# A half row of w2 in eight transfers instead of four, and small work moved off VectorE, in a fused decode step (attention cache and MLP) on one Trainium2 core

## The chip, the cores and the metric

The kernel runs on one core of a Trainium2 chip. The core has TensorE (PE, with its weight loads shown apart as PEld), VectorE (DVE), ScalarE (ACT), GpSimd (POOL) and SyncE (SP), and 16 DMA engines that move data between HBM and the on-chip SBUF. The metric is the device time of one launch in microseconds (us), the median of several runs. The profile is of one execution; its span runs from the first to the last instruction.

## The reference

One decode step for a batch of 2 with one query token each: attention over a cache of 4096 positions, and a GELU MLP, mixed by a gate. Everything is float32.

```python
B, Sq, D = 2, 1, 576
H, Sk, Dh = 32, 4096, 128        # k_cache, v_cache: [B, H, Sk, Dh], 134 MB each
F = 4608                         # w1: [D, F], w2: [F, D], wq: [D, H*Dh], wo: [H*Dh, D]

def _A_ref(x, k_cache, v_cache, wq, wo):
    q = (x @ wq).reshape(B, Sq, H, Dh).transpose(0, 2, 1, 3)
    scores = jnp.einsum("bhqd,bhkd->bhqk", q, k_cache) * (Dh ** -0.5)
    p = _softmax(scores, axis=-1)
    o = jnp.einsum("bhqk,bhkd->bhqd", p, v_cache)
    return o.transpose(0, 2, 1, 3).reshape(B, Sq, H * Dh) @ wo

def _B_ref(x, w1, b1, w2, b2):
    h = _gelu(jnp.einsum("bsd,df->bsf", x, w1) + b1)
    return jnp.einsum("bsf,fd->bsd", h, w2) + b2

g = _sigmoid((x * gate_w).sum(-1, keepdims=True))
return g * _A_ref(...) + (1 - g) * _B_ref(...)
```

## The kernel before

All weights and the whole cache go once through one SBUF tile, `ring`, of three slots of 64 KB a partition. `seq` lists the loads in their order: wq in two pieces and w1 in three, then for each of N = 16 units (one batch entry, four heads) a K block and a V block of 8.39 MB, and last w2 and wo in three groups (`LAST`). `load()` issues the next one on SP's queue. A slot is filled again when the instructions that read it are done. The order of instructions on each engine is that of the code (`manual_schedule`); the framework adds the semaphore waits.

For each unit i, DVE multiplies the K block by the query (`mul`, L510), POOL and DVE reduce it to scores (`red`, L514 to L516), PE and DVE find the maximum (`max_p`, `max_t` with the scaled identity `idsc`, `max_n`), ACT takes the exponentials into the tile `p` and their sums into `rs` (`softmax`, L535), and PE multiplies them with the V block (`av`, L546). That runs one unit behind the products. The front part computes the gate (L270 to L285), the query (L303 with `qps`), and the MLP's hidden layer (L303 with `hps`, L390 to L405), which leaves `hg`, [128 partitions, 36 rows, 2]. The hidden unit that belongs to partition p and row r is 36 p + r, and w2 is read in the same way: row r of w2's tile holds in partition p the weights of unit 36 p + r.

At the end `LAST` brings w2 and wo:

```python
LAST = (
    (("w2", 0, 14), ("w2", 14, 28)),
    (("w2", 28, 36), ("wx", 0, 1), ("wo", 0, 8), ("wo", 8, 16)),
    (("wo", 16, 23), ("wo", 23, 27), ("wo", 27, 30), ("wo", 30, 31), ("wo", 31, 32)),
)
```

Each entry is a transfer of 128 partitions, except that wo's last row comes in four column pieces, and `wx`: this is the second half (288 of 576 columns) of w2's row 35. It is laid out on 16 partitions with XS = 8 weight rows each instead of 128 with one. It is loaded by XC = 4 transfers (L155), each to 4 of the 16 partitions. To multiply it, the 128 x 2 values of `hg`'s row 35 have to be regrouped into `hx`, [16 partitions, 8, 2]: `hx[q, s] = hg[8 q + s, 35]`. Before, DVE does this with two reductions of the identity (`mod`, a mask of p mod 8, and `div`, a mask of p div 8) and a product, PE with one matmul, and DVE copies the result (L407 to L418). `mlp_x` (L421) then multiplies `hx` with `wx` on PE after the other rows of w2, and before wo (`wo_out`, `last_out`).

What sets when a transfer may be issued, beside its slot: the program has eight semaphores for the completion of transfers (named DMAHW0 to DMAHW7 in the rows below), and the transfers of SP's and ACT's queues take them in turn, in the order of the code. A transfer that takes a semaphore again waits until the transfer that had it eight places earlier has landed. SP issues its transfers one after the other, so what stands behind a waiting one waits too.

Of the kernel before, what the change touches and what calls it, by code (L numbers as in the profile page):

```python
# [8 lines left out]
F32 = mybir.dt.float32  # L9
AF = mybir.ActivationFunctionType  # L10
ALU = mybir.AluOpType
AX = mybir.AxisListType
P = 128
# [6 lines left out]
def kernel(  # L20
# [14 lines left out]
    nc = tc.nc  # L35
    B, H, SK, DH = k_cache.shape
# [21 lines left out]
    NF = F // P  # L58
# [4 lines left out]
    SCALE = float(DH) ** -0.5  # L63
# [26 lines left out]
    ps_sm = ctx.enter_context(tc.tile_pool(name="ps_sm", bufs=3, space=bass.MemoryType.PSUM))  # L90
# [18 lines left out]
    def load_w(w, rows, c):  # L109
        if c < len(rows):  # L110
            n = rows[c] * w.shape[1]
            lo = sum(rows[:c]) * P
            src = w[lo:lo + rows[c] * P].rearrange("(p r) n -> p (r n)", r=rows[c])
        else:
            n = w.shape[1] // 2
            src = w[NX * P:].rearrange("q (e n) -> (q e) n", e=2)
        t = ring[:, used["w"]:used["w"] + n]
        used["w"] += n
        nc.sync.dma_start(t, src)
        return t  # L120

    def slot(n):
        k = len(held) % SLOTS
        return ring[:, k * SLOT:k * SLOT + n]

    def load_heads(src, i):

        t = slot(SLOT)
        h = i // B * E
        nc.sync.dma_start(t, src[i % B, h:h + E].rearrange("h (p r) d -> (h p) (r d)", p=PE_))  # L130
        return t.rearrange("p (r d) -> p r d", d=DH)
# [3 lines left out]
    XE, XC = 4, 4  # L135
    XP = XE * XC
    XS = P // XP
    srcx2 = w2.rearrange("(e c s r) n -> c r e s n", e=XE, c=XC, s=XS)[:, NF - 1, :, :, DS:]

    def length(w, a, z):  # L140
        return XS * DS if w == "wx" else (z - a) * D - (DS if (w, z) == ("w2", NF) else 0)

    def load_last(m):
        n = sum(length(*q) for q in LAST[m])

        used["e"], used["z"] = len(held) % SLOTS * SLOT + n, (len(held) % SLOTS + 1) * SLOT
        t = slot(n)
        o = 0
        for w, a, z in LAST[m]:
            if w == "wx":  # L150
                xt = t[:XP, o:o + XS * DS]
                rows[w] = xt.rearrange("p (s n) -> p s n", s=XS)
                o += XS * DS
                for c in range(XC):
                    nc.sync.dma_start(xt[c::XC].rearrange("e (s n) -> e s n", s=XS), srcx2[c])  # L155
                continue
            if (w, z) == ("w2", NF):
                nc.sync.dma_start(t[:, o:o + length(w, a, z)], srcs[w][:, a * D:z * D - DS])
                for r in range(a, z):
                    rows[w, r] = t[:, o + (r - a) * D:o + min((r - a + 1) * D, length(w, a, z))]  # L160
                o += length(w, a, z)
                continue

            ends = (a * D, a * D + DS, a * D + DS + DO, z * D) if (w, z) == ("wo", 32) else (a * D, z * D)
            for u, v in zip(ends, ends[1:]):
                nc.sync.dma_start(t[:, o:o + v - u], srcs[w][:, u:v])
                o += v - u
            for r in range(a, z):
                rows[w, r] = t[:, o - (z - r) * D:o - (z - r - 1) * D]

    def temp(n, parts=P):
        t = ring[:parts, used["t"]:used["t"] + n]
        used["t"] += n
        assert used["t"] <= SLOTS * SLOT
        return t
# [7 lines left out]
    def load():  # L183
        if not seq:
            return
        kind, i = seq.pop()
        if kind == "wq":
            wqt[i] = load_w(wq, ROWS[kind], i)
        elif kind == "w1":
            w1t[i] = load_w(w1, ROWS[kind], i)  # L190
        elif kind == "k":
            kt[i] = load_heads(k_cache, i)
        elif kind == "v":
            vt[i] = load_heads(v_cache, i)
        else:
            load_last(i)
        if kind in ("k", "v", "last"):
            held.append((kind, i))
# [28 lines left out]
    ident = cp.tile([P, P], F32, name="ident")  # L227
    make_identity(nc, ident)
    ones = cp.tile([P, 1], F32, name="ones")
    nc.vector.memset(ones, 1.0)  # L230
    idsc = cp.tile([P, P], F32, name="idsc")
    nc.vector.tensor_scalar_mul(idsc, ident, SCALE)


    NPB = 1
# [3 lines left out]
    pt = []  # L239
    for j in range(NPB):  # L240
        t = cp.tile([P, NT * EB + 32 - EB], F32, name=f"p{j}")
        nc.vector.memset(t, 0.0)
        pt.append(t)
    rs = cp.tile([P, NO], F32, name="rs")
    nc.vector.memset(rs, 0.0)


    sel = ident.rearrange("p (j c) -> p j c", j=4)[:, :, :EB].rearrange("p j (e r) -> p j e r", e=E)
# [70 lines left out]
    to = temp(HG * NO).rearrange("p (f o) -> p f o", f=HG)  # L319
# [69 lines left out]
    for m, ps in enumerate(hps):  # L389
# [7 lines left out]
    hg = cp.tile([P, NF, B], F32, name="hg")  # L397
    t = temp(NF * B).rearrange("p (r b) -> p r b", b=B)
# [5 lines left out]
    nc.vector.tensor_mul(t, t, hb)  # L404
    nc.vector.tensor_mul(hg, t, g1.unsqueeze(1).to_broadcast([P, NF, B]))  # L405

    mod = temp(XS)  # L407
    nc.vector.tensor_reduce(mod, ident.rearrange("p (q s) -> p s q", s=XS), AX.X, ALU.add)
    div = temp(XP)
    nc.vector.tensor_reduce(div, ident.rearrange("p (q s) -> p q s", s=XS), AX.X, ALU.add)  # L410
    hm = temp(XS * B).rearrange("p (s b) -> p s b", b=B)
    nc.vector.tensor_mul(
        hm, hg[:, NF - 1:].to_broadcast([P, XS, B]), mod.unsqueeze(2).to_broadcast([P, XS, B])
    )
    hxps = ps_sm.tile([XP, XS * B], F32, tag="sm", name="hxps")
    nc.tensor.matmul(hxps, div, hm.rearrange("p s b -> p (s b)"), start=True, stop=True)
    hx = cp.tile([XP, XS, B], F32, name="hx")
    nc.vector.tensor_copy(hx.rearrange("p s b -> p (s b)"), hxps)  # L418
    load()

    def mlp_x():  # L421
        for s in range(XS):
# [232 lines left out]
```

## Time and profile before

| | before |
|---|---|
| median of 3 runs | 722.17 us (722.10 to 722.34) |
| profiled execution, its own time | 722.19 us |
| its span | 720.0 us |
| mean granted TensorE clock | 0.663 |
| moved by DMA | 308.84 MB, 429 GB/s over the span |
| busy: DVE, PE, POOL, PEld, ACT | 72%, 33%, 20%, 10%, 5% |

The profile's page shows the busy share of each engine in 40 equal slices, in tenths, and with it the share of the 16 DMA engines. Its DMA queues are q1 (SP's), q10 (ACT's) and two for instructions; packets counts every contiguous piece moved and every write to a completion semaphore. The chain of work that ended last is followed back from the last instruction. The timeline lists instructions by start and duration in us; SPq is SP's queue, and a DMA row there is the issue of a transfer, not its data. A row of windows gives for a stretch of time the busy time of PE, PEld, DVE, ACT and POOL with the number of instructions, then the granted clock, the DMA share and GB/s. A packet is counted in the window in which it starts, so that a share may be over 1.

### The profile page before, as it was taken

The page shows a single profiled execution, that of the slowest core. Times are in us where ns is not written, and L with a number is a line of the kernel's source. Part 1 is how long each engine was busy: PE and PEld are TensorE (multiplying, and loading weights), DVE is VectorE, ACT ScalarE, POOL GpSimd, SP SyncE. Part 2 cuts the span into 40 slices and gives each one's busy share as a digit, 9 for nine tenths or more (in the row PEclk, how much of TensorE's full clock was granted, in tenths as well). Part 3 has the DMA queues.
Part 4 walks back from the last instruction along what each step waited for, and adds up shares of the span by engine and source line. Part 5 has one row for each costly group of instructions (what it writes and reads, how often), then busy time and mean ns, then how long its engine had stood idle before and what let it go on. Part 6 is the DMA issues. An engine that isn't in the chain of part 4 may idle for free.

```text
span 720.0 us, 3946 instructions
## 1 busy us (share of the span) xinstructions
PE 235.7 (33%) x1681; PEld 72.8 (10%) x1681; DVE 518.3 (72%) x154; ACT 37.8 (5%) x141; POOL 143.2 (20%) x28
## 2 busy tenths in 40 slices
PE   0646013140516060604143140506070503223188
PEld 0322000010101010101010010101010101000023
DVE  0003969879696969696969879696969596978900
ACT  0010010100001010101010100101010101010000
POOL 1000040404050403022140404040503113040400
PEclk9967557575757575566657575757575665757599
DMA  9999999999999999999999999999999999999997
GB/s 409 412 443 434 433 437 419 451 420 448 426 448 420 437 437 419 442 430 441 434 433 441 430 431 433 437 430 431 441 430 444 427 444 426 433 430 438 415 426 303
DMA packets 7245, 308.84 MB, mean 429 GB/s; under 512 B 814, under 2 KB 1326, under 8 KB 1596
## 3 DMA queue, kind: packets, MB, share of 16 engines
q1 hardware_dynamic: 7204, 308.55, 99.2%
q8 instruction: 13, 0.21, 0.1%
q10 hardware_dynamic: 24, 0.05, 0.0%
q14 instruction: 4, 0.03, 0.0%
HBM read 308.59 MB, written 0.00 MB: 429 GB/s over the span
## 4 chain that ended last, share of the span: by engine, by line
DMA 45%; DVE 35%; PE 17%; ACT 1%; issue 1%; POOL 0%; ACTq 0%; DVEq 0%; SPq 0%; POOLq 0%
DMA ring<-in_A_k_cache_dram 34%; DVE ring L510 19%; DVE s L515 10%; PE av L546 10%; DMA ring<-in_B_w_dram 5%; DVE s L516 5%; DMA ring<-in_gate_w_dram 3%; DMA ring<-in_A_wo_dram 3%; PE hps L303 2%; PE qps L303 1%; ACT p L535 1%; PE oall L564 1%; DMA ring<-in_B_b_dram 1%; PE mt L525 1%; PE acc L367 1%
## 5 line engine op out<-in xcount | busy, mean ns | idle before, releaser
L510 DVE TENSOR_TENSOR ring<-ring,q 128x16384 f32<-128x16384 f32 x16 | 275.6, 17224 | 100.2 <-DMA ring<-in_A_k_cache_dram 100.2
L514 POOL TENSOR_TENSOR ring<-ring 128x3968 f32<-128x3968 f32 x16 | 137.0, 8564 | 486.9 <-DVE ring L510 419.1
L515 DVE TENSOR_REDUCE s<-ring 128x66 f32<-128x8448 f32 x16 | 143.2, 8953 | 1.3
L546 PE MATMUL av<-ring,p 128*32 128x512 f32 x1024 | 132.6, 676 | 11.4 <-ACT p L535 6.1
L525 PE MATMUL mt<-idsc,m 128*128 128x128 f32 x32 | 12.7, 500 | 359.4 <-DVE m L520 359.4
L516 DVE TENSOR_REDUCE s<-ring 128x62 f32<-128x3968 f32 x16 | 68.4, 4276 | 0.0
L535 ACT ACTIVATE p<-s,bs 32x128 f32<-32x128 f32 x64 | 25.5, 398 | 481.8 <-DVE bs L529 480.6
L546 PEld LDWEIGHTS av<-ring,p 128*32 128x32 f32 x1024 | 35.6, 124 | 118.1 <-issue 101.3
L525 PEld LDWEIGHTS mt<-idsc,m 128*128 128x128 f32 x32 | 8.0, 312 | 375.0 <-DVE m L520 316.7
L351 PE MATMUL qb<-qm,spread 64*128 64x512 f32 x8 | 8.3, 1138 | 71.5 <-POOL qm L347 71.5
L564 PE MATMUL oall<-avs,pick 128*64 128x512 f32 x32 | 30.6, 1059 | 0.8 <-DVE avs L558 0.8
L558 DVE TENSOR_TENSOR avs<-av,selr 128x512 f32<-128x512 f32 x16 | 10.9, 681 | 16.3 <-PE av L546 16.3
L390 DVE TENSOR_TENSOR ring<-hps,ring 128x384 f32<-128x384 f32 x3 | 1.7, 559 | 17.9 <-PE hps L303 17.7
L261 DVE COPY ring<-ring 3x64 f32<-3x64 f32 x2 | 0.3, 182 | 19.2 <-DMA ring<-in_gate_w_dram 19.2
L347 POOL TENSOR_TENSOR qm<-qall,mine 64x512 f32<-64x512 f32 x4 | 4.1, 1032 | 46.3 <-ACT qall L330 46.3
L322 DVE COPY ring<-ident 128x8 f32<-128x8 f32 x8 | 0.7, 171 | 16.8 <-DMA ring<-in_B_b_dram 16.8
L303 PE MATMUL hps<-ring 128*32 128x384 f32 x120 | 11.9, 564 | 0.0
L535 ACT ACTIVATION_READ_ACCUMULATOR p<-s,bs 32x1 f32 x64 | 11.8, 184 | 0.0
L367 PE MATMUL acc<-ring,hg 128*2 128x288 f32 x142 | 10.6, 423 | 1.2 <-DMA ring<-in_B_w_dram 1.2
L303 PE MATMUL qps<-ring 128*32 128x512 f32 x80 | 10.3, 677 | 0.0
L351 PEld LDWEIGHTS qb<-qm,spread 64*128 64x128 f32 x8 | 2.0, 308 | 74.6 <-POOL qm L347 74.6
L481 DVE COPY ring<-res 2x144 f32<-2x144 f32 x1 | 0.3, 297 | 12.4 <-PE res L461 12.4
(92 smaller groups left out, 78.5 us busy)
## 6 DMA issues: line engine op xcount, KB each, us to landing
ring<-in_B_w_dram SPq DMA_DIRECT2D x2, 4608.0 KB
ring<-in_B_w_dram SPq DMA_DIRECT2D x2, 4032.0 KB
ring<-in_A_wo_dram SPq DMA_DIRECT2D x2, 2304.0 KB
ring<-in_B_w_dram SPq DMA_DIRECT2D x1, 2160.0 KB, 13.4
ring<-in_A_wo_dram SPq DMA_DIRECT2D x1, 2016.0 KB
ring<-in_B_w_dram SPq DMA_DIRECT2D x1, 1152.0 KB
ring<-in_A_wo_dram SPq DMA_DIRECT2D x1, 1152.0 KB, 17.6
ring<-in_A_wq_dram SPq DMA_DIRECT2D x1, 1024.0 KB, 24.0
```

Of the source, the lines that this page charges most:

```text
L303: nc.tensor.matmul(ps[32 * j:32 * j + 32, :width], lhs, ts[c][:, o:o + width], start=(k == 0), stop=last, skip_group_check=True,)
L351: nc.tensor.matmul(ps, spread, t.rearrange("p u d -> p (u d)"), start=True, stop=True)
L367: nc.tensor.matmul(acc[o:o + m], lhsT, rhs[:, (s - lo) * DS:(s - lo + 1) * DS], start=start, stop=stop, skip_group_check=True)
L510: nc.vector.tensor_mul(kt[i], kt[i], qs[i].unsqueeze(1).to_broadcast([P, R, DH]))
L514: nc.gpsimd.tensor_add(t[:, :, :DH2], t[:, :, :DH2], t[:, :, DH2:])
L515: nc.vector.tensor_reduce(st[i][:, HALVED:], kt[i][:, HALVED:], AX.X, ALU.add)
L516: nc.vector.tensor_reduce(st[i][:, :HALVED], t[:, :, :DH2], AX.X, ALU.add)
L525: nc.tensor.matmul(mt[i], mx[i].to_broadcast([P, P]), idsc, start=True, stop=True)
L535: nc.scalar.activation(p[w, :, e * RB:(e + 1) * RB], st[i][w].rearrange("p (t c) -> p t c", c=RB), AF.Exp, bias=bias[i][w, e:e + 1], scale ...
L546: nc.tensor.matmul(ps[32 * j:32 * j + 32], p[:, EB * t:EB * t + 32], vt[i][:, RB * t:RB * (t + 1)].rearrange("p r d -> p (r d)"), start=(t ...
L558: nc.vector.tensor_mul(t, avs[i].rearrange("p (r d) -> p r d", d=DH), selr.unsqueeze(2).to_broadcast([P, RB, DH]))
L564: nc.tensor.matmul(oall, pick[:, NO - E - i * E:2 * NO - E - i * E], avs[i].rearrange("p r d -> p (r d)"), start=(i == 0), stop=(i == N - ...
```

## The change

The transfers of `wx` are split in two each: 8 transfers of 4 partitions x 4 weight rows x 288 columns instead of 4 of 4 x 8 x 288. `hx` is made by eight matmuls, one for each s, whose weights are every eighth column of the identity (`ident[:, s::8]`), with `hg`'s row 35 as the moving operand; ACT copies the result out of PSUM. The masks, the product and their temporaries in `ring` are gone, and `load()`, which issues the second K block there, stands ahead of the matmuls. At the start the memsets of `ones`, `p0` and `rs` go from DVE to POOL, and `idsc`, the identity times the scale, from DVE to ACT.

```diff
                 for c in range(XC):
-                    nc.sync.dma_start(xt[c::XC].rearrange("e (s n) -> e s n", s=XS), srcx2[c])
+                    to = xt[c::XC].rearrange("e (s n) -> e s n", s=XS)
+                    for q in range(0, XS, XS // 2):
+                        nc.sync.dma_start(to[:, q:q + XS // 2], srcx2[c][:, q:q + XS // 2])
...
-    nc.vector.memset(ones, 1.0)
+    nc.gpsimd.memset(ones, 1.0)
...
-    nc.vector.tensor_scalar_mul(idsc, ident, SCALE)
+    nc.scalar.mul(idsc, ident, SCALE)
...
-        nc.vector.memset(t, 0.0)
+        nc.gpsimd.memset(t, 0.0)
...
-    nc.vector.memset(rs, 0.0)
+    nc.gpsimd.memset(rs, 0.0)
...
-    mod = temp(XS)
-    nc.vector.tensor_reduce(mod, ident.rearrange("p (q s) -> p s q", s=XS), AX.X, ALU.add)
-    div = temp(XP)
-    nc.vector.tensor_reduce(div, ident.rearrange("p (q s) -> p q s", s=XS), AX.X, ALU.add)
-    hm = temp(XS * B).rearrange("p (s b) -> p s b", b=B)
-    nc.vector.tensor_mul(
-        hm, hg[:, NF - 1:].to_broadcast([P, XS, B]), mod.unsqueeze(2).to_broadcast([P, XS, B])
-    )
-    hxps = ps_sm.tile([XP, XS * B], F32, tag="sm", name="hxps")
-    nc.tensor.matmul(hxps, div, hm.rearrange("p s b -> p (s b)"), start=True, stop=True)
+    load()
+
+    hxps = ps_sm.tile([XP, XS, B], F32, tag="sm", name="hxps")
+    for s in range(XS):
+        nc.tensor.matmul(
+            hxps[:, s], ident.rearrange("p (q s) -> p s q", s=XS)[:, s], hg[:, NF - 1], start=True, stop=True
+        )
     hx = cp.tile([XP, XS, B], F32, name="hx")
-    nc.vector.tensor_copy(hx.rearrange("p s b -> p (s b)"), hxps)
-    load()
+    nc.scalar.copy(hx, hxps)
```

On SP, near the end of the program, the rows of the issues stand as follows before, from the transfer of w2's rows 28 to 35 (128x4320) over the half row (4x8x288) to wo; in brackets the semaphores that a row waits for, those of other engines by the engine's name. The two transfers of w2 ahead of these rows (rows 0 to 13 and 14 to 27) hold semaphores 3 and 4, the one in the first row holds 5.

```order
L158 DMA ring_94<-in_B_w2_dram 128x4320 [waits DMAHW1_49,DVE_49]
L155 DMA ring_94<-in_B_w2_dram 4x8x288 [waits DMAHW2_49]
L155 DMA ring_94<-in_B_w2_dram 4x8x288 x3
L166 DMA ring_94<-in_A_wo_dram 128x4608
L166 DMA ring_94<-in_A_wo_dram 128x4608 [waits DMAHW3_49]
L166 DMA ring_94<-in_A_wo_dram 128x4032 [waits DMAHW4_49,PE_49]
L166 DMA ring_94<-in_A_wo_dram 128x2304 [waits DMAHW5_49,PE_49]
L166 DMA ring_94<-in_A_wo_dram 128x1728 [waits DMAHW6_49,PE_49]
```

And now on SP, at the same place:

```order
L160 DMA ring_94<-in_B_w2_dram 128x4320 [waits DMAHW1_49,DVE_49]
L157 DMA ring_94<-in_B_w2_dram 4x4x288 [waits DMAHW2_49]
L157 DMA ring_94<-in_B_w2_dram 4x4x288 x4
L157 DMA ring_94<-in_B_w2_dram 4x4x288 [waits DMAHW3_49]
L157 DMA ring_94<-in_B_w2_dram 4x4x288 [waits DMAHW4_49]
L157 DMA ring_94<-in_B_w2_dram 4x4x288 [waits DMAHW5_49]
L168 DMA ring_94<-in_A_wo_dram 128x4608 [waits DMAHW6_49]
L168 DMA ring_94<-in_A_wo_dram 128x4608 [waits DMAHW7_49]
L168 DMA ring_94<-in_A_wo_dram 128x4032 [waits DMAHW0_49,PE_49]
```

The waits for semaphores 3, 4 and 5, which stood at the second, third and fourth transfer of wo, now stand at the sixth, seventh and eighth transfer of the half row, ahead of all of wo.

On DVE, behind the hidden layer, before (`hg` is the hidden layer's output times 1 - g, and the rows from L500 on belong to the gate):

```order
L405 TENSOR_TENSOR hg<-ring,g_147 128x72 [waits DVE_49]
L408 TENSOR_REDUCE ring<-ident 128x8
L410 TENSOR_REDUCE ring<-ident 128x16
L412 TENSOR_TENSOR ring<-hg,ring 128x16 [waits DVE_49]
L418 COPY hx<-hxps 16x16 [waits PE_49]
L500 TENSOR_REDUCE gsel<-ident 64x2
```

And now on DVE:

```order
L406 TENSOR_TENSOR ring<-ring 128x72 [waits DVE_49]
L407 TENSOR_TENSOR hg<-ring,g_147 128x72 [waits DVE_49]
L498 TENSOR_REDUCE gsel<-ident 64x2
L501 TENSOR_TENSOR gsel<-gsel,gb 64x2 [waits DVE_49]
L502 TENSOR_REDUCE gall<-gsel 64x1 [waits DVE_49]
```

Four instructions are gone between `hg` and the gate's reduction; the copy of `hx` is now a row on ACT.

## The prediction

> **What bounds the kernel now.** I read the page first (slices, queues, chain), then the chain in time, then SP's issues and fine windows at the end of the stream.
>
> ```profile
> span 720.0 us, 3946 instructions
> DMA  9999999999999999999999999999999999999997
> DMA packets 7245, 308.84 MB, mean 429 GB/s; under 512 B 814, under 2 KB 1326, under 8 KB 1596
> q1 hardware_dynamic: 7204, 308.55, 99.2%
> q10 hardware_dynamic: 24, 0.05, 0.0%
> DMA 45%; DVE 35%; PE 17%; ACT 1%; issue 1%; POOL 0%; ACTq 0%; DVEq 0%; SPq 0%; POOLq 0%
> ```
>
> The 16 DMA engines are busy in every slice but the last. So the kernel is one stream of 308.84 MB; an edit on a compute engine counts only if it makes the stream dry, and a dry stretch cannot be made up later. The chain's DVE share is work that releases a slot while earlier transfers are still queued. At the end the chain is the stream itself:
>
> ```profile
> 692.32 3.50 PE av L546 x32
> 696.19 19.25 DMA ring<-in_A_wo_dram
> 715.48 1.52 PE res L461 x36
> ...
> 716.25:716.50 0.25, 0.25 (x16) 0.07 (x6) 0.00 (x0) 0.00 (x0) 0.00 (x0) 1.00 0.14 44
> 716.50:716.75 0.25, 0.25 (x11) 0.10 (x4) 0.00 (x0) 0.00 (x0) 0.00 (x0) 1.00 0.00 0
> 716.76 0.49 PE L485 MATMUL res<-ring,oP 128*2 128x72 f32 x8
> ```
>
> The first three rows are the chain (start, duration), the next two quarter-microsecond windows (last two columns: DMA share, GB/s), the last the timeline. The last wo packets start before 716.50, and the matmuls that use them start at 716.76: a transfer's data is used 0.25 to 0.5 us behind its last packet. Whatever delays wo delays the end by as much.
>
> **The eight transfers, and the wait they bring.** SP's issues around them, the landing of the w2 transfer ahead (KB, us from issue to landing), and the stream there:
>
> ```profile
> 681.44 0.33 SPq L158 DMA_DIRECT2D ring<-in_B_w_dram  x1
> 682.20 2.84 SPq L155 DMA_DIRECT2D ring<-in_B_w_dram  x4
> 685.08 15.58 SPq L166 DMA_DIRECT2D ring<-in_A_wo_dram  x9
> ...
> ring<-in_B_w_dram SPq DMA_DIRECT2D x1, 2160.0 KB, 13.4
> ring<-in_B_w_dram SPq DMA_DIRECT2D x4, 36.0 KB
> ...
> SPq L166 <- DMA ring<-in_B_w_dram: 4.1, 2, 3.7
> ...
> 690.00:700.00 10.00, 9.19 (x104) 2.88 (x96) 0.74 (x2) 0.00 (x0) 0.00 (x0) 1.00 1.01 428
> ```
>
> Before, the first wo transfer is issued at 685.08, while rows 28 to 35 of w2 land only at 681.44 + 13.4 = 694.84. So wo is queued almost 10 us early, and the DMA engines go over without a gap (share 1.01 from 690 to 700).
>
> Four more issues cost SP 4 x 0.71 = 2.8 us (2.84 for four). Alone that is hidden by those 10 us. But they also take four more of the eight completion semaphores. By the rows of the order (section on the change) the sixth half-row transfer waits for semaphore 3, the seventh for 4, the eighth for 5, on which the three w2 transfers of rows 0 to 35 stand; the row "SPq L166 <- DMA" shows that SP has stood in such waits already, when wo came to those semaphores. The eighth therefore can't be issued before 694.84. Behind it in SP's queue stand all nine wo transfers. When the stream has finished rows 28 to 35 it has only seven half-row transfers of 18 KB each, and then nothing.
>
> How long until wo flows? SP issues the eighth at 694.84, and the first wo after 0.71, at 695.55 (its own semaphore, that of the first half-row transfer, is free by then, since that one is served right behind rows 28 to 35). From an issue into an empty queue to the first packets, two places in the trace:
>
> ```profile
> 0.74 0.87 SPq L119 DMA_DIRECT2D ring<-in_A_wq_dram  x2
> 1.70:1.80 0.10, 0.00 (x0) 0.00 (x0) 0.00 (x0) 0.00 (x0) 0.10 (x2) 1.00 9.71 3277
> 2.40:2.50 0.10, 0.00 (x0) 0.00 (x0) 0.10 (x1) 0.00 (x0) 0.10 (x1) 1.00 1.67 655
> ...
> 717.68 0.29 SPq L491 DMA_DIRECT2D out_dram<-ring  x1
> 718.25:718.50 0.25, 0.00 (x0) 0.00 (x0) 0.00 (x0) 0.00 (x0) 0.00 (x0) 1.00 0.07 18
> ```
>
> A packet is counted where it starts. The first transfer of the program, issued at 0.74, starts its packets from 1.70 to 2.50, that is 0.96 to 1.76 us later; the output's two packets start 0.57 to 0.82 us after their issue. wo has 128 long rows like the first, so I take 1.2 from the front part of that spread: wo flows from 695.55 + 1.2 = 696.75. Before, the last DMA engine passed on to wo when the data of rows 28 to 35 was in, at 694.84 less 0.25 to 0.5, so about 694.45. The stall is 696.75 - 694.45 = 2.3 us. Low end: an issue of 0.33 (as L158's) and 0.57 to the packets, 695.74 against 694.6, so 1.1. High end: 694.84 + 0.71 + 1.76 = 697.31 against 694.35, so 3.0; another 0.5 if the DMA engines that were ahead are the ones missed.
>
> A cross-check by bytes: wo is 4096 x 576 x 4 = 9.44 MB, at the 428 GB/s of the window 22.0 us; 696.75 + 22.0 = 718.8, against 716.5 before: 2.3 again.
>
> The Trainium skill, DMA: Bandwidth & Descriptors, section Latency and other measured facts, gives about 0.6 us to the first byte of a transfer issued by SP. By it the restart is at 696.15 and the sum 1.7 us instead of 2.3; the first transfer's row (0.96 at the earliest) speaks against it, the output's (0.57) for it.
>
> Does PE add to it? In the timeline it multiplies 46 pairs over rows 0 to 22 of wo:
>
> ```profile
> 707.37 5.99 PE L367 MATMUL acc<-ring,oP 128*2 128x288 f32 x92
> ```
>
> That is 0.26 us a row. Rows 16 to 22 are then in at 696.75 + 23/32 x 22.0 = 712.6; PE wants row 16 at 711.5, waits 1.1, and is through at 714.4, before rows 23 to 26 land (696.75 + 27/32 x 22.0 = 715.3). The end stays with the stream, so nothing is added.
>
> **The parts on the compute engines.** The reductions, the product and the copy that leave DVE, beside what surrounds them:
>
> ```profile
> 62.63 0.33 SPq L130 DMA_DIRECT2D ring<-in_A_v_cache_dram  x1
> 69.67 0.23 DVE L405 TENSOR_TENSOR hg<-ring,g 128x72 f32<-128x72 f32 x1
> 69.82 0.38 DVE L408 TENSOR_REDUCE ring<-ident 128x8 f32<-128x128 f32 x1
> 70.53 0.23 PE L416 MATMUL hxps<-ring 128*16 128x16 f32 x2 [5.33 <-DVE ring L412]
> 70.80 0.16 DVE L418 COPY hx<-hxps 16x16 f32<-16x16 f32 x1 [0.33 <-PE hxps L416]
> 70.89 0.33 SPq L130 DMA_DIRECT2D ring<-in_A_k_cache_dram  x1
> 71.38 17.20 DVE L510 TENSOR_TENSOR ring<-ring,q 128x16384 f32<-128x16384 f32 x1
> ...
> 60.00:70.00 10.00, 5.19 (x68) 1.68 (x56) 5.31 (x11) 0.26 (x1) 0.00 (x0) 0.88 0.98 421
> 70.00:80.00 10.00, 0.23 (x2) 0.13 (x2) 9.61 (x8) 0.00 (x0) 0.00 (x0) 0.50 0.97 419
> ```
>
> DVE spends 69.82 to 70.96 on them, so it comes to the first product at most 1.1 us earlier, and the second K load is issued when hg is done, about 69.9 instead of 70.9. The V load issued at 62.63 has 8.39 MB, 19 us of stream, still to move: shares of 0.98 and 0.97 on both sides say that the queue never emptied. Gain: nothing. If the stream had emptied there, it would be at most 1.0 us; the other way there is no loss, as nothing is added ahead of that load.
>
> PE gets eight matmuls, 16 passes, for one of two:
>
> ```profile
> 24.77 2.29 PE L279 MATMUL zps<-ring 128*128 128x2 f32 x10 [0.34 <-DVE ring L275]
> 102.23 0.78 PE mt L525 x2
> ```
>
> By L416 16 x 0.115 = 1.8 us, by L279 (two columns, wider weights) 16 x 0.229 = 3.7 us; either way done by 74, and PE's next work is at 102.23. hx goes through ACT and is wanted at the very end. Nothing.
>
> At the start two rows settle the rest:
>
> ```profile
> 2.33 0.52 DVE L232 TENSOR_SCALAR idsc<-ident 128x128 f32<-128x128 f32 x1 [1.47 <-POOL ident masks.py:199]
> 23.13 0.29 DVE L261 COPY ring<-ring 3x64 f32<-3x64 f32 x2 [19.18 <-DMA ring<-in_gate_w_dram]
> ```
>
> DVE stood 19.18 us for the gate load, so it had the time for idsc and memsets; they save nothing. On POOL and ACT they fall into the same wait; ACT's own transfers stand ahead of idsc in its queue, and idsc is first read by PE at 102.23. If that cover were gone they would cost about what they did on DVE, the half microsecond of the row each. Sum: +2.3, all of it from semaphores.
>
> **The rivals.** (a) The wait is there but short: SP's issue and the restart come near the low end, 1.1 to 1.4 us. For it: the output's 0.57. Against: that transfer has two packets, and the first one, like wo, took 0.96 at the earliest. Time 723.3 to 723.6, no change that a measurement can tell. (b) The stall is larger: the DMA engines end rows 28 to 35 at different times, all then wait for the slowest, and PE falls behind too. The end shares (0.14 in the last window) say that some end early and few late, so the lost lead costs little if the last one stays the last. Time 725.7 to 727. (c) Faster: eight transfers spread over more DMA engines. Before, the queue's 7204 packets are 49 transfers of 128 rows with 16 completions (7056), the output's 2 + 2, and 144 left, that is 128 half-rows and 16 completions, four a transfer: four engines carry 147 KB, 36.9 KB each, at 428/16 = 26.8 GB/s 1.4 us. On 16 engines it would be 0.35, a gain of 1.0 us if those four end last. It decides only if the stall is under 1.0, so if wo flows before 695.5, and it is to be had only if a transfer of four partitions were to change its four engines. ACT's queue has 24 packets for 12 short rows, as if each took one completion of its own: partitions set the number. Time 721.2 with no stall at all.
>
> The Trainium skill, same page, section Why a DMA increments its semaphore by 16 and not by 1, says that the engine count is the largest number up to 16 that divides the slowest dimension of both sides, four here before and after. The counts of packets agree, so (c) gets little.
>
> **How the numbers follow.** The forecast has 0.80, (a) 0.09, (b) 0.08, (c) 0.03. The profiled execution took 722.19 for a span of 720.0; the median of the runs is 722.17, so the sum can be set on either: 722.2 + 2.3 = 724.5. The range takes the bounds, 1.1 to 3.5: 723.3 to 725.7. A measurement of this kernel tells some 0.2%, 1.44 us, from no change, so slower starts at 723.6: forecast and (b), 0.88; same 0.09; faster 0.03.
>
> **What would show it.** Right: SP issues seven half-row transfers by about 690, the eighth at 694.8 and the first wo at about 695.5; the DMA share has a hole of about 2 us between 694 and 697; the stream's last packet is near 718.8 instead of 716.5, with the rest of the end as before. q1 would count 16 packets more (7220). The second K load goes out near 69.9 with nothing else moved. Wrong: the first wo issued near 688, so that the semaphores did not bind (the time is then 722.2); or a hole earlier, at 35 to 115, where K and V loads change places with slots; or an end in which PE, not wo, is last.

## The result and the profile after

The changed kernel takes 726.07 us (median of six runs, 726.01 to 726.95) against 722.18 before (six runs as well): the ratio is 1.0056, 95% interval 1.0043 to 1.0069. It is slower by 3.9 us. Forecast were 2.3 us slower, 724.5, in a range up to 725.7: the sign and the place are right, the size is not, and the time lies outside the range. The profiled execution took 726.06 for a span of 724.3.

The page after: span, DMA share in 40 slices, packets of SP's queue.

```profile
span 724.3 us, 3981 instructions
DMA  9999999999999999999999999999999999999987
q1 hardware_dynamic: 7220, 308.55, 98.7%
```

The second slice from the end is no longer full, and q1 has the 16 packets more that four transfers to four DMA engines each bring. SP's issues at that place (start, duration), and its waits there:

```profile
689.56 5.73 SPq L157 DMA_DIRECT2D ring<-in_B_w_dram  x2
695.33 0.91 SPq L168 DMA_DIRECT2D ring<-in_A_wo_dram  x2
...
SPq L157 <- DMA ring<-in_B_w_dram: 7.4, 2, 4.5
```

The seventh half-row transfer is issued at 689.56. The eighth ends its issue at 689.56 + 5.73 = 695.29, and the first wo transfer follows at 695.33, where it was 685.08 before. SP waits twice for w2 transfers ahead of the half row's, 4.5 us the second time. Windows over the hole this makes, first of 1 us, then some of 0.2 us (last two columns: DMA share, GB/s):

```profile
693.00:694.00 1.00, 1.00 (x16) 0.26 (x8) 0.00 (x0) 0.00 (x0) 0.00 (x0) 1.00 0.24 89
694.00:695.00 1.00, 1.00 (x12) 0.26 (x8) 0.00 (x0) 0.00 (x0) 0.00 (x0) 1.00 0.00 0
695.00:696.00 1.00, 1.00 (x16) 0.39 (x12) 0.00 (x0) 0.00 (x0) 0.00 (x0) 1.00 0.00 0
696.00:697.00 1.00, 1.00 (x16) 0.26 (x9) 0.00 (x0) 0.00 (x0) 0.00 (x0) 1.00 1.31 313
...
696.40:696.60 0.20, 0.20 (x8) 0.03 (x4) 0.00 (x0) 0.00 (x0) 0.00 (x0) 1.00 4.02 922
696.80:697.00 0.20, 0.20 (x8) 0.06 (x4) 0.00 (x0) 0.00 (x0) 0.00 (x0) 1.00 0.34 92
697.00:697.20 0.20, 0.20 (x8) 0.04 (x4) 0.00 (x0) 0.00 (x0) 0.00 (x0) 1.00 0.00 0
```

wo's first rows start between 696.4 and 697.0 (the few packets ahead of 696.4 are the eighth half-row transfer); the forecast had 696.75. But the packets that start from 696 to 697 have a share of 1.31 for 313 GB/s, where the window from 690 to 700 before had 1.01 for 428: each takes 1.31/313 over 1.01/428, 1.8 times as long. And the end of the stream:

```profile
719.50:720.00 0.50, 0.15 (x8) 0.13 (x12) 0.00 (x0) 0.00 (x0) 0.00 (x0) 1.00 0.14 37
720.00:720.50 0.50, 0.50 (x24) 0.40 (x16) 0.00 (x0) 0.00 (x0) 0.00 (x0) 1.00 0.12 37
720.50:721.00 0.50, 0.50 (x20) 0.11 (x8) 0.00 (x0) 0.00 (x0) 0.00 (x0) 1.00 0.10 32
721.00:721.50 0.50, 0.50 (x16) 0.29 (x12) 0.04 (x1) 0.00 (x0) 0.00 (x0) 1.00 0.01 2
```

A share of 0.12 is two DMA engines of 16. Fourteen are done by 719.5, two work on alone for 1.5 us, and the end waits for them. Before, the last packets started ahead of 716.50.

### The profile page after: what moved, and what is told of

Its sections match the earlier page's. It is cut to its first block, busy times and chain, and to the rows that moved or that the text cites. A ratio compares the mean times of both kernels' runs of the same rounds, so it can differ in the third digit from the quotient of the medians.

```text
span 724.3 us, 3981 instructions
## 1 busy us (share of the span) xinstructions
PE 238.5 (33%) x1695; PEld 73.7 (10%) x1695; DVE 517.0 (71%) x146; ACT 38.3 (5%) x143; POOL 143.8 (20%) x31
## 3 DMA queue, kind: packets, MB, share of 16 engines
q1 hardware_dynamic: 7220, 308.55, 98.7%
## 4 chain that ended last, share of the span: by engine, by line
DMA 49%; DVE 34%; PE 14%; ACT 1%; issue 1%; POOL 0%; SPq 0%; ACTq 0%; DVEq 0%; POOLq 0%
DMA ring<-in_A_k_cache_dram 38%; DVE ring L508 19%; PE av L544 10%; DVE s L513 10%; DMA ring<-in_B_w_dram 5%; DVE s L514 5%; DMA ring<-in_A_wo_dram 3%; DMA ring<-in_gate_w_dram 3%; PE qps L305 1%; ACT p L533 1%; PE oall L562 1%; PE mt L523 1%; PE acc L369 0%; DVE m L518 0%; PE zps L281 0%
## 5 line engine op out<-in xcount | busy, mean ns | idle before, releaser
L544 PE MATMUL av<-ring,p 128*32 128x512 f32 x1024 | 135.2, 687 | 11.4 <-ACT p L533 6.2
```

The lines of the kernel that those rows point to most:

```text
L544: nc.tensor.matmul(ps[32 * j:32 * j + 32], p[:, EB * t:EB * t + 32], vt[i][:, RB * t:RB * (t + 1)].rearrange("p r d -> p (r d)"), start=(t ...
```

## The experiments

### Which edit it is

Four kernels: the change without the eight transfers, the eight transfers without the change, and six and seven transfers instead of eight.

e1_four:

```diff
-                    for q in range(0, XS, XS // 2):
-                        nc.sync.dma_start(to[:, q:q + XS // 2], srcx2[c][:, q:q + XS // 2])
+                    nc.sync.dma_start(to, srcx2[c])
```

> The changed kernel with the half row back in four transfers; the rest of the change (memsets on POOL, idsc and hx on ACT, eight matmuls, the second K load ahead of them) stays. Theory S (the whole loss comes from the eighth transfer waiting for semaphore 5): 722.2 within 0.3, SP's first wo issue back near 685, no hole in the stream. Rival C (the edits on the compute engines bring a part, through the order of PE's work or where its instructions are fetched): between 723 and 726.

Measured: 721.83 us, ratio to before 0.9995 (0.9986 to 1.0005). SP's first wo issue is back at 685.34.

e2_eight_only, against the kernel before:

```diff
-                    nc.sync.dma_start(xt[c::XC].rearrange("e (s n) -> e s n", s=XS), srcx2[c])
+                    to = xt[c::XC].rearrange("e (s n) -> e s n", s=XS)
+                    for q in range(0, XS, XS // 2):
+                        nc.sync.dma_start(to[:, q:q + XS // 2], srcx2[c][:, q:q + XS // 2])
```

> The kernel before with the half row in eight transfers and nothing else. Theory S: about 726.0, the first wo issue near 695.3. Rival C: 723 to 725, because the eight transfers alone bring the 2.3 us of the prediction and the rest of the change the other 1.6.

Measured: 726.06 us, ratio 1.0054 (1.0039 to 1.0069), with the hole between 694 and 696. So the eight transfers bring all of it, and the memsets, `idsc`, the eight matmuls, the copy on ACT and the earlier K load bring nothing that can be told from zero.

e3_six and e4_seven, with 2 and 3 for N (the number of the four transfers that are split):

```diff
-                    for q in range(0, XS, XS // 2):
-                        nc.sync.dma_start(to[:, q:q + XS // 2], srcx2[c][:, q:q + XS // 2])
+                    w_ = XS // 2 if c < N else XS
+                    for q in range(0, XS, w_):
+                        nc.sync.dma_start(to[:, q:q + w_], srcx2[c][:, q:q + w_])
```

> The changed kernel with six transfers (two of the four split). The last of the six waits for semaphore 3, the first wo transfer for 4, whose w2 transfer lands near 689.6, 3 us before the first DMA engine runs out. Theory S: 722.2 within 0.3. Rival N (each added transfer costs by itself, 3.9 us for four): 724.1.

> The changed kernel with seven transfers (three of the four split). Now the first wo transfer itself waits for semaphore 5, so it is issued near 694.7 instead of 695.3. Theory S: 726.1 less one issue of 0.67, 725.4. Rival N: 725.1 (2.9 of 3.9), to be told from S only together with six: N has a step of 1.0 from six to seven, S one of 3.2.

Measured: six 721.77 us (ratio 0.9994, 0.9985 to 1.0004), seven 725.38 (1.0046, 1.0029 to 1.0063). SP's issues with six, and a window of it where the hole was:

```profile
682.27 4.16 SPq L158 DMA_DIRECT2D ring<-in_B_w_dram  x6
689.35 0.34 SPq L169 DMA_DIRECT2D ring<-in_A_wo_dram  x1
...
694.00:695.00 1.00, 1.00 (x16) 0.34 (x12) 0.00 (x0) 0.00 (x0) 0.00 (x0) 1.00 1.09 465
```

And with seven:

```profile
689.61 0.62 SPq L158 DMA_DIRECT2D ring<-in_B_w_dram  x1
694.73 1.85 SPq L169 DMA_DIRECT2D ring<-in_A_wo_dram  x4
```

Four to six transfers cost nothing, the seventh costs 3.6 us, the eighth the 0.7 of its own issue. A price per transfer is out. What decides is at which transfer the wait for semaphore 5 comes: with six at the second of wo, when the first (issued at 689.35) keeps the DMA engines fed; with seven at the first of wo.

### Why 3.9 and not 2.3

The part that the forecast lacks is behind the restart. In the changed kernel two 16 KB pieces of the instruction queue are fetched while wo flows, each one packet on one DMA engine (queue, packets, MB, share of 16 engines from 697 to 719.4):

```profile
q1 hardware_dynamic: 1199, 9.08, 96.5%
q8 instruction: 2, 0.03, 0.5%
```

0.5% of 16 x 22.4 us is 1.8 us, 0.9 a piece. The theory (F below): after the hole all engines start wo within 0.6 us of each other, and each piece then makes one of them late; two pieces, two late engines. The pieces are PE's instructions, as the runs below bear out: they move with PE's work, and with less of it there are 12 of them in the whole run instead of 13. To take them out of that stretch, two kernels leave work out on PE.

e5_cut_eight and, in the same way against the kernel before, e6_cut_four:

```diff
-    mlp_out(24, 30)
     norm_t()
-    mlp_out(30, 33)
     o_turn(turn)
-    mlp_out(33, NF)
-    mlp_x()
-    wo_out(0, FOLD)
     last_out()
...
-        for r in range(FOLD, 31):
+        for r in (FOLD, FOLD + 3, 29, 30):
```

> The changed kernel with eight transfers, but without part of PE's work at the end: rows 24 to 35 of w2, the half row, rows 0 to 22 of wo and rows 24, 25, 27 and 28 of wo are loaded and not multiplied (194 of PE's passes left out; the output lacks these rows). Theory F (behind the restart of the stream all DMA engines run level, and each 16 KB piece of PE's instructions that is fetched then makes one engine some 1.4 us late; two such pieces set the end): no piece is fetched behind 693 any more, no engine is late, the DMA share drops to zero within 0.5 us at the end, and the time is 1.5 us shorter, 724.5. Rival G (the late engines are late for another reason, such as the short rows of the last transfers or PE reading beside them): 726.0 within 0.3.

> The kernel before (four transfers) with the same work left out on PE. Theory F: there the engines enter wo up to 3 us apart, and the pieces fetched behind 694 fall on engines that are ahead; the last one runs through without a piece, so the end stays: 722.2 within 0.4. Rival H (the pieces, or PE's work, set the end there too): 720.7 to 721.3, and the whole loss between this run and the one before it stays 3.9. By F that difference shrinks to 2.3.

Measured: eight 725.07 us, 1.0 less than the full one; four 722.50 (ratio 1.0004, 0.9995 to 1.0014). PE has 186 passes fewer by the page, not 194. There is no row of q8 for 697 to 719.4 in the shortened kernel with eight transfers, and its end is

```profile
719.50:720.00 0.50, 0.50 (x16) 0.27 (x8) 0.00 (x0) 0.00 (x0) 0.00 (x0) 0.54 0.11 32
720.00:720.50 0.50, 0.39 (x12) 0.10 (x4) 0.23 (x1) 0.19 (x1) 0.00 (x0) 1.00 0.00 0
```

No engine is late. The gain is 1.0 instead of the 1.5 that F expected. PE's clock, which is at half here until shortly before 720 (0.54 in the first of these windows, 1.00 in the full kernel), may have a part in that; no run measured it. The gap between eight and four transfers falls from 3.9 to 2.57 us. That fits F, but the work left out could be the cause as well. So the shortened kernel with eight transfers was given matmuls near 72 us, to shift the place in the program where the next piece is fetched.

```diff
-    for s in range(XS):
+    for s in [0] * M + list(range(XS)):
```

> The shortened kernel with eight transfers (the same work left out at the end of PE), with 32 matmuls more on PE near 72 us, where PE has nothing to do until 102. They repeat the first of the eight that make hx, so nothing is computed anew; they only move the point in the program at which PE's next 16 KB of instructions are fetched, by half a piece. Theory F: one piece is now fetched between 697 and 716, behind the restart, one DMA engine ends some 1.4 us behind the other 15, and the time is 1.0 to 1.4 us longer than without the shift (725.07), 726.1 to 726.5. Rival G (the late engines came from the work left out): 725.1 within 0.2.

> The shortened kernel with eight transfers and 16 matmuls more near 72 us instead of 32. With 32 the piece fell ahead of the restart, at 693.19, so no engine was late and the two theories were not told apart; without any it fell at 719.44, when the stream was over. A quarter of a piece should put it between 700 and 717. Theory F: one DMA engine ends 1.4 us behind the others (a DMA share of about 0.06 for more than a microsecond at the end), and the time is 1.0 to 1.4 us longer than 725.1: 726.1 to 726.5. Rival G: 725.1 within 0.2.

> The same with 8 matmuls more: the piece should fall between 716 and 719, still ahead of the end of the stream. Theory F: again one late engine, 726.0 to 726.5, the same as with 16, since it doesn't matter where behind the restart an engine loses its 1.4 us. Rival G: 725.1 within 0.2.

> The shortened kernel with 20 matmuls more near 72 us. With 0, 8 and 16 the last piece of PE's instructions came at 719.44, 719.24 and 719.63, as the stream ended, with 32 at 693.19, ahead of the restart; so somewhere between 16 and 32 it crosses the stretch of wo. Theory F holds for whichever of 20, 24 and 28 has its piece between 695 and 718: a DMA share near 0.06 for over a microsecond at the end, and 1.0 to 1.4 us more than 725.05. One that has it outside: 725.05 within 0.2. Rival G: all three at 725.05 within 0.2, wherever the piece falls.

> The same with 24 matmuls more, the middle of the three: the likeliest to have its piece between 695 and 718. Theory F: 726.05 to 726.45. Rival G: 725.05 within 0.2.

> The same with 28 matmuls more. Theory F: 726.05 to 726.45 if its piece falls between 695 and 718, otherwise 725.05 within 0.2. Rival G: 725.05 within 0.2.

Measured, with M of 32, 16, 8, 20, 24 and 28: 725.11, 725.00, 725.04, 725.11, 725.18 and 725.02 us. All six are where rival G put them, and none supports F. In their traces the piece starts at 693.19, 719.63, 719.24, 695.94, 694.88 and 694.05: with eight and sixteen matmuls at the end of the stream, with more ahead of the restart or in the hole, never while all engines are on wo. In five of them the piece is not where F needs it, so they tell nothing. With 20 it is, by the words of the expectation: 695.94 lies between 695 and 718, for which F gave 726.05 to 726.45, and F missed. That piece ended at 697.23 and lay for the most part in the hole: its engine started on wo at 697.22, the others between 696.5 and 696.9. That this spared it was concluded afterwards. I had taken the place to move in step with PE's passes, and it jumps. So the piece was put there in another way: with more work for PE inside the stretch, where it waits anyway.

e13_cut_more_pe, and e14_four_more_pe the same on the shortened kernel with four transfers:

```diff
     o_turn(turn)
+    more = ps_sm.tile([XP, B], F32, tag="sm", name="more")
+    for _ in range(48):
+        nc.tensor.matmul(more, ident.rearrange("p (q s) -> p s q", s=XS)[:, 0], hg[:, NF - 1], start=True, stop=True)
     last_out()
```

> The shortened kernel with eight transfers, and 48 matmuls (96 passes of PE, about 4 us) into a tile that nobody reads, put where PE waits from 704 to 716.6. The shifts of 0 to 32 matmuls all left the piece of instructions outside 697 to 719 and the time at 725.0 to 725.2. With 96 passes more inside that stretch a piece must be fetched in it, near 708. Theory F: one engine 1.4 us late (DMA share near 0.06 for a microsecond or more at the end) and 1.0 to 1.4 us more than 725.1: 726.1 to 726.5. Rival G: 725.1 within 0.2, since PE is done with them 8 us before it is wanted.

> The shortened kernel with four transfers and the same 48 matmuls more. Theory F: a piece falls into the same stretch, but the engines run up to 3 us apart there and it makes an engine late only if it hits one of the last; 15 of 16 say that the time stays at 722.5 within 0.3. If it hits the last one, 723.5 to 723.9. Rival G: 722.5 within 0.3 as well; only e13 tells F from G, this one tells whether the fetch costs the kernel before as much.

Measured: eight 726.51 us, 1.44 more than without the matmuls; four 722.45, no different from 722.50. The queue from 697 to 719.4 and the end of the one with eight:

```profile
q1 hardware_dynamic: 1141, 9.09, 96.7%
q8 instruction: 1, 0.02, 0.3%
...
719.50:720.00 0.50, 0.14 (x4) 0.00 (x0) 0.00 (x0) 0.00 (x0) 0.00 (x0) 0.50 0.23 74
720.00:720.50 0.50, 0.46 (x8) 0.11 (x8) 0.00 (x0) 0.00 (x0) 0.00 (x0) 0.50 0.06 21
720.50:721.00 0.50, 0.48 (x12) 0.11 (x8) 0.00 (x0) 0.00 (x0) 0.00 (x0) 0.50 0.07 23
```

One piece, one engine late (0.06 is one of 16), and its lateness in the time. A small part of the 1.44 may be PE's: its clock is at 0.50 in all these windows, and at 1.00 from 720 on in the kernel without the matmuls. With four transfers a piece falls into the same stretch too (queue from 697 to 716.5):

```profile
q1 hardware_dynamic: 1194, 7.58, 92.6%
q8 instruction: 1, 0.02, 0.3%
```

and costs nothing: the engines come to wo far apart there (between 691.4 and 694.3 in this trace), and the one with the piece was not the last. The full kernel with only the eight transfers (e2) says the same from its side: one piece in the stretch (the next starts at 719.92, at the end), and one engine late:

```profile
q8 instruction: 1, 0.02, 0.3%
...
720.00:720.50 0.50, 0.39 (x16) 0.34 (x20) 0.00 (x0) 0.00 (x0) 0.00 (x0) 1.00 0.07 25
```

With one late engine e2 takes 726.06 us, and the changed kernel with two 726.07: the end waits for the last engine, so the pieces do not add up.

The packets themselves, which the traces hold with start, duration and size, show it engine by engine. They name no engine, but an engine's next packet starts as its last one ends, so that it can be followed. In the changed kernel the two engines that take the pieces at 706.94 and 718.62 end at 721.07 and 720.78, the other fourteen between 719.0 and 719.5. With the 48 matmuls (e13) the engine with the piece ends at 721.08, the others by 719.8. The piece takes 0.94 us there, and the row of wo behind it 1.19 us instead of 0.69, so that this engine is 1.4 us late. In the kernel before, the engine with the piece at 707.50 had come to wo at 692.99 and the last engine at 694.41, and the stream ends at 716.53: the lead of 1.4 us was just enough. With four transfers and the 48 matmuls (e14) it was the same, 692.95 against 694.32.

### One transfer instead of four

Since four transfers and six cost the same, one might be better than both kernels: it frees semaphores and spreads the half row over 16 DMA engines.

```diff
-    srcx2 = w2.rearrange("(e c s r) n -> c r e s n", e=XE, c=XC, s=XS)[:, NF - 1, :, :, DS:]
+    srcx2 = w2.rearrange("(q s r) n -> r q s n", q=XP, s=XS)[NF - 1, :, :, DS:]
...
-                for c in range(XC):
...
+                nc.sync.dma_start(rows[w], srcx2)
```

> The changed kernel with the half row in one transfer of 16 partitions x 8 rows, so that 16 DMA engines take it instead of four. Three semaphores fewer are taken than with four transfers. Theory S has no wait here, so nothing of the loss. The four engines that took 1.5 us of it are not the last ones by the trace (they enter wo by 694.1, the last at 694.4), so moving it gives nothing and puts 0.35 us on the last one: 722.0 to 722.3. Rival (the four do end last): 720.8 to 721.3, faster than both kernels.

Measured: 723.57 us, ratio 1.0020 (1.0011 to 1.0029), so slower than four transfers by 1.7, and both expectations missed. The stream slows where the half row stands in it:

```profile
692.00:693.00 1.00, 1.00 (x20) 0.43 (x16) 0.00 (x0) 0.00 (x0) 0.00 (x0) 1.00 1.04 296
693.00:694.00 1.00, 1.00 (x16) 0.26 (x8) 0.00 (x0) 0.00 (x0) 0.00 (x0) 1.00 1.14 219
694.00:695.00 1.00, 1.00 (x13) 0.26 (x9) 0.00 (x0) 0.00 (x0) 0.00 (x0) 1.00 0.90 210
```

The engines are busy, but move half as much. One guess was neighbouring partitions; e9_adjacent has four transfers to four neighbours each:

```diff
-                    to = xt[c::XC].rearrange("e (s n) -> e s n", s=XS)
+                    to = xt[c * XE:(c + 1) * XE].rearrange("e (s n) -> e s n", s=XS)
```

(with the source's e and c exchanged, and one transfer for each c as in e1_four).

> The changed kernel with four transfers whose four partitions are next to each other (4c to 4c+3) instead of four apart; bytes, semaphores and engines per transfer as with four. It asks why one transfer of 16 partitions lost 1.7 us. Theory A (DMA engines that write to neighbouring partitions share a way into SBUF and slow each other, rows in flight with them too): slower than four transfers (721.83) by 1 to 3 us, the GB/s falling between 692 and 696. Rival B (16 engines with eight short rows each are what costs): 721.8 within 0.3.

Measured: 721.97 us, ratio 0.9997 (0.9988 to 1.0007), and the stream at

```profile
693.00:694.00 1.00, 1.00 (x12) 0.26 (x8) 0.00 (x0) 0.00 (x0) 0.00 (x0) 1.00 1.10 440
694.00:695.00 1.00, 1.00 (x16) 0.32 (x12) 0.00 (x0) 0.00 (x0) 0.00 (x0) 1.00 1.01 418
```

So neighbours alone are not it. That 16 engines take short rows at once is one thing that remains, but no run shows it; the cause stays open.

No kernel here beats the one before by more than its measurement tells: six transfers and four with the rest of the change are 0.4 us below it with intervals that hold 1 (and some 0.1 us below the 721.9 to 722.5 that theory S gave for both).

## Why the prediction was right or wrong

**The wait** was right. The eighth transfer stood until semaphore 5 was free, with all of wo behind it; the first wo issue came at 695.33 (695.55 in the forecast), and the step from six to seven transfers shows that it is this wait and not the number of issues.

**The restart** was right: first rows from 696.4 to 697.0 (696.75). From wo's issue that is 1.1 us at the earliest; with seven transfers (e4), where nothing of the half row stands just ahead of wo, the issue is at 694.73 and the first rows start at 695.70, so 0.97. The Trainium skill, DMA: Bandwidth & Descriptors, section Latency and other measured facts, has about 0.6 us to the first byte; the traces have more both at the program's start (0.96) and behind the hole, where a long transfer starts into an empty queue, so here the measurement decides.

**The step that failed** is "Whatever delays wo delays the end by as much", by which the sum was the stall and nothing else, and the cross-check by bytes that was to confirm it: "at the 428 GB/s of the window 22.0 us; 696.75 + 22.0 = 718.8". It let all engines run at full rate at once and end level. Fourteen end by 719.5, the last at 721.1. Two terms were missing. The first rows behind the hole took 1.8 times as long; the 313 KB of that window need 1.31 us an engine instead of 313/428 = 0.73, so 0.6. That with the stall was measured as 2.57 us, the gap between the shortened kernels, against 2.3 forecast, which leaves 2.0 for the stall itself. Read from the packets it is 2.2 (the last engine came to wo at 694.41 before, the first rows now start at 696.6 in the mean), so that term was right. And the engines did not end level: two of them 1.5 us behind, because of instruction pieces. That is the rest of the 3.9, 1.3 us. That it is the pieces is shown by e13 against e5 (1.44 us for one piece), and by the packets of the late engines; that the first rows are slow is seen in the traces only, and why they are is open.

**Rival (b)** had the time, 725.7 to 727, and the place, that engines run apart and lose their lead, but not the mechanism. PE did not fall behind (its matmuls at 719.85 had waited for wo), and the lost lead was argued away: it "costs little if the last one stays the last". Before, a piece could fall on an engine that was ahead, and e14 shows it free. After the hole no engine is ahead, so a single piece on any of them delays the end by its full 1.4 us, and a second one on another engine adds nothing. No term of (b) holds that; that its range covers 726.07 is luck in good part.

**The parts on the compute engines** were right at nothing: e1 and e2 differ from before and after by less than 0.4 us. PE got its sixteen passes, in less time than the 1.8 us of the low bound:

```profile
68.12 0.69 PE L413 MATMUL hxps<-hg,ident 128*16 128x2 f32 x16 [4.76 <-DVE hg L407]
68.26 0.33 SPq L130 DMA_DIRECT2D ring<-in_A_k_cache_dram  x1
```

The second K load goes out at 68.26, not 69.9, since the whole front was earlier in this execution, and moved nothing else.

**Rivals (a) and (c)** did not come. For (c), q1's 7220 packets say four engines a transfer as before, as the Trainium skill, DMA: Bandwidth & Descriptors, section Why a DMA increments its semaphore by 16 and not by 1, has it. In e7, with one transfer on 16 engines, there were 1.7 us of loss and not 1.0 of gain.

Between span and time there are 2.2 us in the profiled execution before and 1.8 after, so the spans differ by 4.3 and the times by 3.9. What makes these 0.4 us is not known.

## What to carry to other kernels

When a transfer is split, count the completion semaphores: the cost is not the issue but which old transfer each later one then waits for, and what stands behind it in the queue; six transfers were free here, seven cost 3.6 us. And a stream that runs dry loses more than the hole: the restart's first rows are slow, and the engines' head starts, which had taken up small disturbances for nothing, are gone.

## What the runs showed of the hardware

A 16 KB piece of PE's instructions takes one DMA engine for 0.9 to 1.0 us, and the row behind it 1.15 to 1.19 us instead of 0.69 (changed kernel, e2, e13), so that the engine is some 1.4 us late. In a level stream that was 1.44 us of time (e13 against e5), and nothing where the engines came to wo up to 3 us apart and the one hit was ahead by 1.4 us (e14 against e6). The first rows behind the hole took 1.8 times the usual time. One transfer of 16 partitions x 8 rows of 1152 B slowed the stream around it from about 430 to 210 to 300 GB/s for 3 us, where four transfers of 4 partitions did not.
